# PSUM as eight single banks, a bank for fillers, an earlier identity and a new order table in a linear-attention and squared-ReLU kernel

## The chip, the cores and the metric

The kernel runs on one core of one Trainium2 chip. The metric is the device time of one execution in microseconds; the runs of the kernel before gave 358.99, 359.10 and 359.19 us, median 359.1.

## The reference

Attention with an exponential feature map and no softmax, then a feed-forward network (FFN):

```python
def phi(x):                                   # q, k: (8, 8, 576, 64), w_phi: (64, 128)
    proj = einsum('bhsd,df->bhsf', x, w_phi)
    proj = proj - max(abs(proj), axis=-1, keepdims=True)
    return concatenate([exp(proj), exp(-proj)], axis=-1)
q_p, k_p = phi(q), phi(k)
kv = einsum('bhsf,bhsd->bhfd', k_p, v)
z = sum(k_p, axis=2)
x = einsum('bhsf,bhfd->bhsd', q_p, kv) / (einsum('bhsf,bhf->bhs', q_p, z)[..., None] + 1e-06)
x = x.transpose(0, 2, 1, 3).reshape(4608, 512)
h = maximum(x @ w_in, 0.0)                    # w_in: (512, 2048)
out = (h * h @ w_out)                         # w_out: (2048, 512)
```

Inputs and output are float32; the matrix work is done in bfloat16.

## The kernel before

**Stages.** For each of the 8 batches, `k_batch` (L582) transposes k (on TensorE for batches 0 and 1, L630; by DMA transposes on the SP queue later), projects it against w_phi (L660), takes the largest magnitude per row on VectorE (L595) and both exponentials on ScalarE (L602); `em` holds the exponentials of the maxima (L704), `va` and `var` the products of v with them (L755, L738) with a column of ones beside them (L716, L720); the key-value sums go to PSUM (L776, L781) and are copied to `kvs`. `q_batch` (L811) does the same with q: transposes (L840), one projection for the maximum (L878, reduced by L925), one for the exponentials (L888, L915), the numerators and denominators (L970), their two halves added (L1009, L1013), the division (L1032, L1042), and the transpose of the result into `xT` (L1083, or by DMA).

The 36 output tiles of 128 rows are taken in chunks: four of one tile, then 16 of two. `hp_chunk` multiplies `xT` by w_in in groups of 512 PSUM columns (L1133), evicts each group with a ReLU on ScalarE (L1151) or VectorE (L1153), and squares it into `h` (L1161, L1163). `op_chunk` multiplies `h` by w_out (L1189), evicts (helper `copy`, L417 on ScalarE, L419 on VectorE) and stores each tile from the SP queue. The last tile is computed as two halves of 256 columns.

**Order.** Every operation is an `Op` with the engines that may run it. `ORDER` is a table of operation numbers, in which they are emitted; a negative number puts the operation on the second engine of its list. Each engine runs its instructions in that order. A ring (`Ring`) is a set of buffers; the table's order also decides which buffer an operation takes, and a buffer that is taken again makes the taker wait for its last reader.

**PSUM.** `r_pj` has three buffers of two banks (projections, numerators, key-value sums), `r_mo` two buffers of one bank (transposes, both FFN products, batch 0's key-value sums).

**Fillers.** `warm` (L391) issues matmuls on a constant ahead of an operation, into the buffer which that operation is about to fill; `WARM` says how many units of 128 columns, by operation number (57 in all). One operation of 40 more units stands in batch 0. 24 units on zeros open the program.

**Loads.** They are issued by GpSimd (Pool), which converts to bfloat16 on the way: first k's heads 2, 3, 6, 7 of batch 0 (`emit_heads`, L488; the others come from the SP queue as float32 and are cast), then v whole (L467), then the identity is built, the last rows of k and v (L477), and `FIRST` (q in halves L470, w_in in four parts L526), then `SECOND` (k, w_out L531, q, v). For batch 0 Pool also writes the ones of `var` (L720).

Of the kernel before, what the change touches and what calls it, by code (L numbers as in the profile page):

```python
# [17 lines left out]
ORDER = (  # L18
# [208 lines left out]
def kernel(  # L227
# [34 lines left out]


    EARLY = 2


    XB_IN, XB_X = 2, 2

# [966 lines left out]
    for o in plan.order():  # L1235
        if o.emit:
            o.emit(o)
# [30 lines left out]
```

## Time and profile before

| | |
|---|---|
| runs (median) | 359.1 us |
| span of the profiled execution | 358.4 us |
| around the span, against the median | 0.7 us |
| TensorE busy | 346.4 us, mean granted clock 0.990 |
| VectorE / ScalarE busy | 292.4 / 262.9 us |
| GpSimd busy | 58.5 us |
| first L1133 matmul, first L1189 matmul | 28.4 us, 40.1 us |
| HBM read and written | 36.77 MB, 9.44 MB |

The profiled execution's own time is given as its span. The page of the profile lists busy time by engine, slices of the span, the chain of work that ended last, and groups of instructions by source line. Line numbers in what follows are those of the kernel before, unless a changed line is meant. A row of the timeline has the start, the length, the engine, the line, the operation, output and inputs, the count of merged instructions, and in brackets the idle time ahead and what ended it.

### The profile page before, as it was taken

Reading aid. Unit: us, or ns where it says so; the run is one execution under the profiler, and the core shown is the slowest. Engines: PE = TensorE matmul, PEld = TensorE weight load, DVE = VectorE, ACT = ScalarE, POOL = GpSimd, SP = SyncE. Lnnn points to the kernel's source line nnn. Section 1 sums busy time; section 2 is a strip of 40 time slices with the busy share of each in tenths; the row PEclk is TensorE's granted clock in tenths of the full one; section 3 lists DMA queues with packets and bytes.
Section 4 is the critical chain, followed back from the end, with each engine's and each line's share of the span. In section 5 each row is a group of like instructions: output and inputs, shape, how many; then the busy total and the mean of one; then the engine's idle time right before and its main releaser. Section 6 shows DMA issues by size and latency. Waiting matters only on the chain.

```text
span 358.4 us, 9254 instructions
## 1 busy us (share of the span) xinstructions
PE 346.4 (97%) x3860; PEld 239.1 (67%) x3894; DVE 292.4 (82%) x529; ACT 262.9 (73%) x436; POOL 58.5 (16%) x88
## 2 busy tenths in 40 slices
PE   8699999999999999999999999999999999999995
PEld 4378667775776676767576757757685768576754
DVE  5979998889998998788988699979988988591310
ACT  4979997996798774698849883798879867544641
POOL 8643323442160113100220002000000000000000
PEclk9969999999999999999999999999999999999999
DMA  9999999999997499607982194435203001113011
GB/s 161 185 197 207 194 208 141 170 181 187 186 152 138 83 171 150 107 15 145 124 126 53 59 149 96 61 89 82 60 16 88 18 35 48 65 34 88 2 59 59
DMA packets 92281, 39.33 MB, mean 110 GB/s; under 512 B 59728, under 2 KB 87760, under 8 KB 92240
## 3 DMA queue, kind: packets, MB, share of 16 engines
q0 software_dynamic: 42752, 18.09, 42.7%
q1 hardware_dynamic: 49328, 20.59, 28.6%
q8 instruction: 30, 0.49, 0.6%
q10 hardware_dynamic: 160, 0.07, 0.1%
q14 instruction: 11, 0.09, 0.1%
HBM read 36.77 MB, written 9.44 MB: 129 GB/s over the span
## 4 chain that ended last, share of the span: by engine, by line
PE 82%; DVE 8%; ACT 7%; issue 1%; POOL 1%; ACTq 0%; POOLq 0%
PE mo L1133 32%; PE mo L1189 31%; PE pj L781 4%; PE pj L970 4%; ACT kph L602 4%; PE pj L878 3%; PE pj L888 2%; DVE m L595 2%; PE pj L660 2%; DVE tmp L1009 1%; ACT hr L1151 1%; PE pj L776 1%; PE mo L781 1%; DVE va L755 1%; DVE hr L1153 1%
## 5 line engine op out<-in xcount | busy, mean ns | idle before, releaser
L1133 PE MATMUL mo<-xT,win 128*128 128x256 bf16 (+1 forms) x1280 | 139.3, 262 | 0.8 <-ACT hr L1151 0.2
L1189 PE MATMUL mo<-wout,h 128*128 128x512 bf16 (+1 forms) x558 | 131.2, 373 | 1.8 <-issue 0.2
L1133 PEld LDWEIGHTS <-win 128*128 128x128 bf16 x1280 | 111.3, 98 | 19.7 <-issue 4.3
L1189 PEld LDWEIGHTS <-h 128*128 128x128 bf16 x592 | 54.5, 98 | 57.3 <-issue 2.8
L915 ACT ACTIVATE qph<-pj 128x1024 bf16<-128x1024 f32 (+1 forms) x80 | 72.8, 940 | 11.6 <-PE pj L888 11.6
L1151 ACT ACTIVATE hr<-mo 128x512 bf16<-128x512 f32 x99 | 58.7, 598 | 28.2 <-PE mo L1133 27.0
L602 ACT ACTIVATE kph<-pj 128x1024 bf16<-128x1024 f32 (+1 forms) x80 | 71.2, 949 | 6.4 <-PE pj L660 4.9
L1163 DVE TENSOR_TENSOR h<-hr 128x512 bf16<-128x512 bf16 x82 | 33.7, 419 | 22.6 <-ACT hr L1151 22.0
L925 DVE TENSOR_REDUCE mq<-pj 128x8 f32<-128x1024 f32 (+1 forms) x40 | 44.2, 1108 | 4.5 <-PE pj L878 4.4
L595 DVE TENSOR_REDUCE m<-pj 128x8 f32<-128x1024 f32 (+1 forms) x40 | 44.3, 1111 | 3.4 <-ACT kph L602 1.7
L1161 ACT ACTIVATE h<-hr 128x512 bf16<-128x512 bf16 x62 | 38.9, 631 | 8.3 <-DVE hr L1153 7.5
L755 DVE TENSOR_TENSOR va<-vin,em 128x512 bf16<-128x512 bf16 x63 | 40.2, 683 | 0.1
L1153 DVE TENSOR_SCALAR hr<-mo 128x512 bf16<-128x512 f32 x45 | 30.6, 684 | 7.9 <-PE mo L1133 7.4
L417 ACT ACTIVATE ot<-mo 128x512 f32<-128x512 f32 (+1 forms) x24 | 14.0, 585 | 25.1 <-PE mo L1189 25.1
L1009 DVE TENSOR_TENSOR tmp<-pj,e 128x520 f32<-128x520 f32 x31 | 21.1, 692 | 6.1 <-PE pj L970 6.1
L970 PEld LDWEIGHTS <-qph 128*128 128x128 bf16 x512 | 21.9, 98 | 5.4 <-issue 1.5
L1042 DVE TENSOR_TENSOR xo<-tmp,rden 128x512 bf16<-128x512 f32 (+1 forms) x39 | 24.3, 631 | 0.5
L970 PE MATMUL pj<-kvs,qph 128*128 128x65 bf16 x512 | 24.4, 194 | 0.2
L781 PEld LDWEIGHTS <-kph 128*128 128x128 bf16 x512 | 21.5, 101 | 0.3
L1013 DVE TENSOR_TENSOR tmp<-pj,tmp 128x520 f32<-128x520 f32 x31 | 21.2, 692 | 0.5 <-PE pj L970 0.4
L781 PE MATMUL pj<-va,kph 128*128 128x65 bf16 x448 | 18.4, 194 | 0.0
L467 POOL DMA_DIRECT2D vin<-in_v_dram x8 | 7.2, 895 | 68.5 <-DVE va L755 63.1
(75 smaller groups left out, 268.5 us busy)
## 6 DMA issues: line engine op xcount, KB each, us to landing
out_dram<-ot SPq DMA_DIRECT2D x31, 256.0 KB, 2.4
vin<-in_v_dram POOLq DMA_DIRECT2D x8, 512.0 KB, 9.0
kin<-in_k_dram POOLq DMA_DIRECT2D x7, 512.0 KB, 11.9
qin<-in_q_dram POOLq DMA_DIRECT2D x7, 512.0 KB, 10.3
win<-in_moe_w_in_dram POOLq DMA_DIRECT2D x4, 512.0 KB, 10.1
wout<-in_moe_w_out_dram POOLq DMA_DIRECT2D x2, 1024.0 KB, 14.8
out_dram<-ot SPq DMA_DIRECT2D x10, 128.0 KB, 2.4
xT<-xo SPq DMA_TRANSPOSE x36, 2.6
```

What stands on the lines that cost most here:

```text
L595: nc.vector.tensor_reduce(out=st["m"].rearrange("p (n c) -> p c n", c=2)[:, :, n0 : n0 + n], in_=st["pj", g][:, :, :n], axis=AX.X, op=ALU. ...
L602: nc.scalar.activation(out=st["kph"][:, s, n0 : n0 + n].rearrange("p n c f -> p c n f"), in_=st["pj", g][:, :, :n], func=ACT.Exp, scale=1. ...
L755: nc.vector.tensor_tensor(out=st["va"][:, s, gs, 0:D], in0=tiles["v", b].rearrange("p h i d -> p (h i) d")[:, gs, :], in1=st["em"][:, s, g ...
L781: nc.tensor.matmul(out=kv[:, sum_of(h) - 2 * prs[0], :], lhsT=st["kph"][:, s, 2 * h + i // 2, i % 2, :], rhs=st["va"][:, s, h * NI + i, :] ...
L915: nc.scalar.activation(out=st["qph", pt][:, s, half, n0 : n0 + n], in_=in_, func=ACT.Exp, scale=1.0 - 2.0 * s)
L925: nc.vector.tensor_reduce(out=st["mq", pt][:, half, n0 : n0 + n], in_=in_, axis=AX.X, op=ALU.max, apply_absolute_value=True)
L970: nc.tensor.matmul(out=nps[:, n + 4 * (ab or 0), :], lhsT=qph[:, s, half, sl, :], rhs=kvs[:, s, sum_of(sl), :], start=True, stop=True)
L1133: nc.tensor.matmul(out=hp[:, mi, :], lhsT=win[:, kc, mc * P : (mc + 1) * P], rhs=st_x[c][:, kc, 0:nt, :], start=kc == kcs[0] and (ab is No ...
L1151: nc.scalar.activation(out=out_, in_=in_, func=ACT.Relu)
L1153: nc.vector.tensor_scalar(out=out_, in0=in_, scalar1=0.0, scalar2=None, op0=ALU.max)
L1161: nc.scalar.activation(out=out_, in_=hr, func=ACT.Square)
L1189: nc.tensor.matmul(out=st["op"], lhsT=hst["h2"][:, mc, tt * P : (tt + 1) * P], rhs=wout[:, mc, cols], start=(mc == 0), stop=(mc == KC2 - 1))
```

## The change

PSUM becomes one ring of eight single banks, `r_ps`. A projection that took a buffer of two banks takes two banks, each with its own reductions and exponentials; the numerators are computed in groups of four heads in one bank, with sums of 260 columns; the key-value sums of every batch come in two parts. Fillers go to the first bank, which the first operation takes and which is given back by the first FFN product; they stand ahead of an operation in the order, with new counts (187 units in all), and are always matmuls of up to 512 columns.

The identity is built before any load. v of batch 0 is loaded as two halves of the heads, with k's last rows between them; the ones of `var` leave Pool for VectorE or ScalarE. w_phi comes in one transfer to both halves of the partitions, and one copy makes its bfloat16 form.

ReLU outputs of two neighbouring groups share a buffer (three of 2 x 512 instead of four of 512), and one instruction squares both; the last chunk stays as it was. The last tile is computed as 384 and then 128 columns. `load_gate` is there and not used (`GATED` is False). `ORDER` has 2078 numbers instead of 1718, all of them new; it also sets anew which engine takes the evictions, squares and copies, and the order of the loads: after batch 2's k and q, Pool issues k of batches 3 and 4 and then v of batch 2.

```diff
-    r_pj = Ring("pj", 3, [P, 2, 4, P], F32, pool=ps)
-    r_mo = Ring("mo", 2, [P, 4, P], F32, pool=ps)
+    r_ps = Ring("ps", 8, [P, 4, P], F32, pool=ps)
...
-    r_hr = Ring("hr", 4, [P, 512], BF16)
+    r_hr = Ring("hr", 3, [P, 2, 512], BF16)
...
     def c_w2(op):
-        for half in range(2):
-            rows = slice(half * Dh, (half + 1) * Dh)
-            copy(op, w2[rows, half], wst[rows])
+        copy(op, w2, wst)
...
-            nc.scalar.dma_start(out=wst[half * Dh : (half + 1) * Dh], in_=w_phi)
+        nc.scalar.dma_start(out=wst, in_=w_phi.unsqueeze(0).to_broadcast([2, Dh, Fd]))
...
     def e_first(op):
-        warm(r_pj.tile(op)[:, 0], WARM_UP, zero)
+        spare["t"] = r_ps.tile(op)
+        fill(WARM_UP, zero)
+
+    def fill(n, with_):
+        for m in [4] * (n // 4) + ([n % 4] if n % 4 else []):
+            nc.tensor.matmul(out=spare["t"][:, :m], lhsT=with_, rhs=with_.unsqueeze(1).to_broadcast([P, m, P]),
                              start=True, stop=True)
...
+            o_id.follow(after)
             o1, lb = plan.issue("sw", 2, key, {"pool": (1.7, 1.75)}, emit_heads, "kB", (), [r_in[name].slots],
-                                after=[after])
-            o3, l3 = load("v", 0, key)(o1)
-            o_id.follow(o3)
-            o2, l2 = rest(o3)
-            o2.follow(o_id)
+                                after=[o_id])
+            o_v, d_v, o = None, [], o1
+            for n in range(2):
...
+                    nc.gpsimd.dma_start(out=tiles["v", 0].rearrange("p h i d -> p h (i d)")[:, hs],
+                                        in_=v[0, hs, 0:SM, :].rearrange("h (p i) d -> p h (i d)", i=NI))
...
+                if n == 0:
+                    o2, l2 = rest(o)
...
+            for par in range(2):
+                lock = Lock()
+
+                def e_red(op, g=g, n0=n0, n=n, par=par):
+                    nc.vector.tensor_reduce(
+                        out=st["m"].rearrange("p (n c) -> p c n", c=2)[:, par, n0 : n0 + n], in_=st["pj", g, par][:, :n],
+                        axis=AX.X, op=ALU.max, apply_absolute_value=True)
...
+                        nc.scalar.activation(out=st["kph"][:, s, n0 : n0 + n, par, :], in_=st["pj", g, par][:, :n],
+                                             func=ACT.Exp, scale=1.0 - 2.0 * s)
...
+                        for hg in (0, 1) if ab is None and pt < 2 else (0,):
+                            heads = (2 * ab, 2 * ab + 1, 2 * ab + 4, 2 * ab + 5) if first_tile else range(4 * hg, 4 * hg + 4)
+                            holds = [Hold(r_ps.slots) for _ in range(1 if pt < 2 else 2)]
...
+            pair = c < len(CHUNKS) - 1
+            at, upto = (g % 2, g % 2) if pair else (0, 1)
...
+            gives += [] if chain["hp"] else [(r_ps.slots, o_first)]
...
-            wide = DM // 2 if t0 + tt == NT - 1 else DM
-            for c0 in range(0, DM, wide):
+            for c0, wide in [(0, 3 * P), (3 * P, P)] if t0 + tt == NT - 1 else [(0, DM)]:
...
     for o in plan.order():
+        if o.warm:
+            fill(o.warm, ident)
         if o.emit:
             o.emit(o)
```

More of the change, by code (lines that the diff above doesn't have):

```diff
@@ L264 @@
     EARLY = 2
-    XB_IN, XB_X = 2, 2
+    GATED = False
+    XB_IN, PE_X = 2, [(b, pt, half) for b in range(2) for pt in range(3) for half in range(2)]
     def sum_of(h):
@@ new lines, in k_batch, with e_kp @@
+        for g in groups:
+            key = kd - 6.0 - 2.2 * (4 - g)
+            holds = [Hold(r_ps.slots) for _ in range(2)]
+            def e_kp(op, g=g, holds=holds):
+                if g == 0:
+                    st["kph"], st["m"] = r_kph.tile(op), r_m.tile(op)
+                n0, n = GROUPS[g]
+                pj = [r_ps.tile(hold) for hold in holds]
+                st["pj", g, 0], st["pj", g, 1] = pj
+                for u in range(n):
+                    for par in range(2):
+                        rows = slice(par * Dh, (par + 1) * Dh)
+                        nc.tensor.matmul(out=pj[par][:, u, :], lhsT=st["kT"][rows, n0 + u, :], rhs=w2[rows, :],
+                                         start=True, stop=True)
+            o_kp = add(key - 1, {"pe": mm(P, GROUPS[g][1])}, e_kp, [cp_ops[g], o_w2],
+                       holds + ([r_kph.slots, r_m.slots] if g == 0 else []),
@@ L866, in q_batch @@
                 key = xk - 9.0 + (12 if split else 1) * pi
-                hm, hq = Hold(r_pj.slots), Hold(r_pj.slots)
-                size = 256 * w
+                hm, hq = ([Hold(r_ps.slots) for _ in range(2)] for _ in range(2))
+                banks = [(half, 4 * bank, 4) if split else (bank, n0, n) for bank in range(2)]
                 def e_qm(op, pt=pt, pi=pi, mms=mms, w=w, hm=hm):
-                    pj = st["pm", pt, pi] = r_pj.tile(hm)
+                    pj = st["pm", pt, pi] = [r_ps.tile(hold) for hold in hm]
                     if pi == 0:
                         st["mq", pt] = r_mq.tile(op)
-                    warm(pj[:, 0], op.warm)
                     for u in range(w):
@@ L877, in e_qm @@
                             rows = slice(par * Dh, (par + 1) * Dh)
[L878 to L879 removed]
+                            nc.tensor.matmul(out=pj[bank][:, u, :], lhsT=q_blocks(st, pt, blk + u, 1)[rows, 0],
+                                             rhs=w2[rows, :], start=True, stop=True)
                 def e_qp(op, pt=pt, pi=pi, mms=mms, w=w, hq=hq):
[L882 removed]
+                    pj = st["pq", pt, pi] = [r_ps.tile(hold) for hold in hq]
@@ L907, in q_batch @@
-                if split and pi:
-                    late = o_qm, o_qp
-                o_mq, o_q0 = o_mq or o_qm, o_q0 or o_qp
-                for s in range(2):
-                    def e_exp(op, pt=pt, pi=pi, half=half, n0=n0, n=n, w=w, s=s):
-                        in_ = st["pq", pt, pi][:, :, :w]
-                        if n == 8:
-                            in_ = in_.rearrange("p a b t -> p (a b) t")
-                        nc.scalar.activation(out=st["qph", pt][:, s, half, n0 : n0 + n], in_=in_, func=ACT.Exp,
-                                             scale=1.0 - 2.0 * s)
-                    exps.setdefault(pi, []).append(add(key + 2.5 + 0.2 * s, {"act": act(size)}, e_exp, [o_qp],
-                                                       give=[(r_pj.slots, hq)]))
@@ L921, in e_red @@
-                def e_red(op, pt=pt, pi=pi, half=half, n0=n0, n=n, w=w):
-                    in_ = st["pm", pt, pi][:, :, :w]
-                    if n == 8:
-                        in_ = in_.rearrange("p a b t -> p (a b) t")
-                    nc.vector.tensor_reduce(out=st["mq", pt][:, half, n0 : n0 + n], in_=in_, axis=AX.X, op=ALU.max,
-                                            apply_absolute_value=True)
-                reds.append(add(key + (3.5 if b == 0 else 0.5), {"dve": dve(size)}, e_red, [o_qm], give=[(r_pj.slots, hm)]))
+                o_qm = add(key, {"pe": mm(P, w * (1 + split))}, e_qm, need + [o_w2], hm + first[:1], give=qT_give,
+                           after=[o_mq], mode="row")
@@ new lines, in q_batch, with e_exp, e_red @@
+                o_qp = add(key + (0.1 if b else 2), {"pe": mm(128 * w, 1 + split)}, e_qp, need + [o_w2], hq + first[1:],
+                           give=qT_give, after=[o_q0], mode="row")
+                o_mq, o_q0 = o_mq or o_qm, o_q0 or o_qp
+                mine = []
+                for bank, (half_, h0, nh_) in enumerate(banks):
+                    for s in range(2):
+                        def e_exp(op, pt=pt, pi=pi, bank=bank, half_=half_, h0=h0, nh_=nh_, w=w, s=s):
+                            nc.scalar.activation(out=st["qph", pt][:, s, half_, h0 : h0 + nh_],
+                                                 in_=st["pq", pt, pi][bank][:, :w], func=ACT.Exp, scale=1.0 - 2.0 * s)
+                        exps[half_, h0, s] = add(key + 2.5 + 0.2 * s, {"act": act(128 * w)}, e_exp, [o_qp],
+                                                 give=[(r_ps.slots, hq[bank])])
+                    def e_red(op, pt=pt, pi=pi, bank=bank, half_=half_, h0=h0, nh_=nh_, w=w):
+                        nc.vector.tensor_reduce(out=st["mq", pt][:, half_, h0 : h0 + nh_], in_=st["pm", pt, pi][bank][:, :w],
+                                                axis=AX.X, op=ALU.max, apply_absolute_value=True)
+                    mine.append(add(key + (3.5 if b == 0 else 0.5), {"dve": dve(128 * w)}, e_red, [o_qm],
+                                    give=[(r_ps.slots, hm[bank])]))
@@ L1147, in e_hr, with e_hp @@
-            def e_hr(op, mcs=mcs):
-                st["hr", mcs[0]] = r_hr.tile(op, [P, gm, nt * P])
-                out_, in_ = st["hr", mcs[0]], st["hp", mcs[0]]
+            def e_hp(op, mcs=mcs):
+                hp = st["hp", mcs[0]] = r_ps.tile(op, [P, gm, nt * P], [None, None, nt * P])
+                if "h2" not in st:
+                    st["h2"] = r_h2.tile(op)
+                for mi, mc in enumerate(mcs):
+                    for kc in range(KC1):
+                        nc.tensor.matmul(out=hp[:, mi, :], lhsT=win[:, kc, mc * P : (mc + 1) * P],
+                                         rhs=st_x[c][:, kc, 0:nt, :], start=kc == 0, stop=kc == KC1 - 1)
@@ new lines, in hp_chunk @@
+            xs = [o for t in range(t0, t0 + nt) for o in x_ops[t]]
+            gives = [(r_xT.slots, xt_take[c])] if mcs[-1] == KC2 - 1 else []
+            gives += [] if chain["hp"] else [(r_ps.slots, o_first)]
+            o_hp = add(key, {"pe": mm(nt * P, 4 * gm)}, e_hp, xs + [d_win[mcs[-1] * P * WPARTS // DF]],
+                       [r_ps.slots] + ([] if o_h2 else [r_h2.slots]), give=gives, after=[chain["hp"]])
+            chain["hp"] = o_hp
+            o_h2 = o_h2 or o_hp
+            pair = c < len(CHUNKS) - 1
```

390 lines of the change are left out of this document (154 added, 236 removed), and 193 rows, old and new, of tables (ORDER, WIRE).

## The prediction

> **What bounds the kernel now.** First the page: busy shares, clock, chain.
>
> ```profile
> span 358.4 us, 9254 instructions
> PE 346.4 (97%) x3860; PEld 239.1 (67%) x3894; DVE 292.4 (82%) x529; ACT 262.9 (73%) x436; POOL 58.5 (16%) x88
> ...
> PEclk9969999999999999999999999999999999999999
> ...
> PE 82%; DVE 8%; ACT 7%; issue 1%; POOL 1%; ACTq 0%; POOLq 0%
> ```
>
> TensorE carries 82% of the chain that ended last, but its 97% includes fillers and matmuls that run slowly or wait half-filled. The clock dips in slices two and three only. So I cut the span into stretches: up to the first FFN matmul, up to where the chain becomes nearly all TensorE, and a late attention stretch.
>
> ```profile
> 0.00:28.40 28.40, 23.21 (x250) 14.72 (x250) 22.40 (x45) 20.27 (x44) 18.25 (x32) 0.88 1.29 182
> 28.40:92.00 63.60, 62.07 (x824) 43.65 (x829) 58.84 (x111) 55.11 (x94) 21.07 (x30) 1.00 1.48 182
> ...
> 172.80:246.40 73.60, 73.08 (x822) 49.92 (x829) 65.61 (x115) 55.93 (x88) 6.39 (x9) 1.00 0.56 94
> ```
>
> Columns: length, then busy time (count) of PE, PEld, DVE, ACT, POOL, clock, DMA share, GB/s. The first 28.4 us do almost no FFN work. From there to 92 us VectorE has 63.6 - 58.84 = 4.8 us free, so it paces that stretch as much as TensorE does. Later (172.8 to 246.4) VectorE has 8 us and ScalarE 17.7 us free, and TensorE sets the pace.
>
> **The start: identity first.** The timeline of all engines:
>
> ```profile
> 1.24 1.56 POOL L488 DMA_DIRECT2D kin<-in_k_dram  x2 [0.80 <-POOLq L1252]
> ...
> 3.62 0.45 DVE L419 CAST kin<-h 128x256 bf16<-128x256 f32 x1 [0.36 <-DMA h<-in_k_dram]
> 3.67 0.25 POOL masks.py:197 MEMSET ident<- 128x128 bf16 x1
> ...
> 4.00 0.29 POOL masks.py:199 TENSOR_SCALAR_AFFINE_SELECT ident<-ident 128x128 bf16<-128x128 bf16 x1
> ...
> 4.34 0.93 PE L396 MATMUL mo<-ident 128*128 128x128 bf16 x7 [0.61 <-POOL ident masks.py:199]
> ...
> 5.07 0.63 PE L630 MATMUL mo<-ident,kin 128*128 128x128 bf16 x4
> ...
> 5.49 1.24 PE L400 MATMUL pj<-ident 128*128 128x512 bf16 x3
> ...
> 6.67 0.40 PE L660 MATMUL pj<-w,kT 64*128 64x128 bf16 x8
> ...
> 7.11 1.23 DVE L595 TENSOR_REDUCE m<-pj 128x8 f32<-128x1024 f32 x1 [0.75 <-PE pj L660]
> ```
>
> k is cast by 3.62 + 0.45 = 4.07, yet its transposes start at 5.07: the identity ends at 4.29, then come seven fillers; three more (1.24 us) precede the projection. Identity first moves its 0.62 us (3.67 to 4.29) to about 1.24, and shrinks those fillers to about 0.5 us. Transposes at 4.1, copy at 4.8, projection at 5.3, reduction at 5.7: **1.4 us** earlier than 7.11. The price: k's other heads and every load queued behind them on Pool start 0.62 us later, which costs 0 to 0.62; v is now two issues around k's rows, about 0.8 us of Pool each. w_phi in one transfer and one copy is needed only by that projection, and is hidden behind the casts; uncovered it costs its one copy, at most the 0.45 of the cast.
>
> **The start: fillers in a bank of their own.** Before, each filler needed the bank of the operation that it precedes, so none could run while banks were held. Two-microsecond stretches, TensorE's timeline, then two pieces of the chain at full clock, the starts of one key-value group and the next:
>
> ```profile
> 18.00:20.00 2.00, 2.00 (x23) 1.46 (x22) 2.00 (x6) 2.00 (x9) 0.68 (x2) 0.50 1.34 202
> 20.00:22.00 2.00, 2.00 (x27) 1.80 (x27) 1.92 (x4) 1.51 (x2) 0.82 (x1) 0.50 1.24 206
> ```
>
> ```profile
> 16.66 0.93 PE L878 MATMUL pj<-w,qT 64*128 64x128 bf16 x8 [1.97 <-DVE m L595]
> ...
> 21.57 0.65 PE L781 MATMUL mo<-va,kph 128*128 128x65 bf16 x8
> ...
> 22.12 0.65 PE L781 MATMUL mo<-va,kph 128*128 128x65 bf16 x8
> ...
> 28.41 1.96 PE L1133 MATMUL mo<-xT,win 128*128 128x128 bf16 x32
> ```
>
> ```profile
> 59.09 0.06 PE pj L776
> ...
> 59.39 0.06 PE pj L776
> ```
>
> TensorE is idle for 1.97 us until a VectorE reduction frees a pair; then the granted clock is 0.50. A key-value group takes 22.12 - 21.57 = 0.55 us there, 59.39 - 59.09 = 0.30 at full clock. Six such groups lose 1.5 us, the projections and transposes between (0.93 against 0.40 for eight) about 1.5 more: 0 to 3 us. The new order has 187 units of filler (128 columns each) against 97, nearly all before the first FFN matmul, in their own bank; at 1.96 / 32 = 0.06 us a unit (L1133 above) that is 11 us, put where TensorE waits. At half clock they would be 22, and late work would queue behind them.
>
> How much of it counts is VectorE's sum. Its timeline:
>
> ```profile
> 14.03 0.68 DVE L595 TENSOR_REDUCE m<-pj 128x4 f32<-128x512 f32 x1
> 14.63 0.74 DVE L419 COPY qT<-mo 128x512 bf16<-128x512 bf16 x2
> ...
> 20.42 2.35 DVE L925 TENSOR_REDUCE mq<-pj 128x8 f32<-128x1024 f32 x2
> 23.91 0.43 DVE L419 COPY qT<-mo 128x512 bf16<-128x512 bf16 x1 [1.14 <-PE mo L840]
> 24.91 0.76 DVE L1001 TENSOR_TENSOR tmp<-pj,e 128x260 f32<-128x260 f32 x2 [0.58 <-PE pj L970]
> ...
> 27.17 0.69 DVE L1009 TENSOR_TENSOR tmp<-pj,e 128x520 f32<-128x520 f32 x1
> 27.78 0.48 DVE L419 COPY xT<-mo 128x256 bf16<-128x256 bf16 x2
> ```
>
> Before, 7.11 to 28.26 is 21.15 us, some 2.7 of them idle (1.14 and 0.58 behind slow TensorE). Steps, start to start: a 512 reduction 0.60, a 1024 one 2.35 - 1.23 = 1.12, 260 columns at most 0.38 (two in 0.76), 520 columns 0.61, a qT copy 0.74 - 0.43 = 0.31. The changed order has 12 reductions of 512 and 2 of 256, 10 products for v (0.60), 4 copies of k, 4 sums of 260, and small ones: 7.9 + 6.0 + 1.2 + 1.5 + 1.7 = 18.3 us. From 5.7 this gives 24.0 without a wait, 26.7 with the old idle time. With 1.2 us of waits and 0.5 for later loads the first FFN matmul is at 25.8: **-2.6 us**; bounds -4.4 (no waits) and -0.8.
>
> Can it be kept? The second FFN matrix decides:
>
> ```profile
> L1189 PE MATMUL mo<-wout,h x558: 272/379/391, 40.1 to 354.5; 128*128 128x512 bf16 x176, 128*128 128x256 bf16 x10
> L531 POOL DMA_DIRECT2D wout<-in_moe_w_out_dram x2: 878/885/892, 19.9 to 22.5; - x2
> ...
> DMA to landing us min/median/max: 13.4/14.8/16.1
> ```
>
> Its halves land at 33.3 to 36.0 and 35.9 to 38.6 and are first used from 40.1; 2.6 us earlier is 37.5, for the first half. It just fits.
>
> **Single banks.** Two exponentials of 1024 become four of 512, reductions and numerator sums are halved. ScalarE's prices:
>
> ```profile
> 168.07 1.02 ACT L915 ACTIVATE qph<-pj 128x1024 bf16<-128x1024 f32 x1
> ...
> 169.08 1.08 ACT L1151 ACTIVATE hr<-mo 128x512 bf16<-128x512 f32 x2
> ...
> 170.90 0.60 ACT L1151 ACTIVATE hr<-mo 128x512 bf16<-128x512 f32 x1 [0.22 <-PE mo L1133]
> ...
> 173.92 1.93 ACT L915 ACTIVATE qph<-pj 128x1024 bf16<-128x1024 f32 x2
> ```
>
> Steps: 1.08 - 0.60 = 0.48 and 1.93 - 1.02 = 0.91; a split costs 2 x 0.48 - 0.91 = 0.05 back to back, at most 0.17 by whole durations. 160 splits: 8 us (at most 27). With 26 more squares moved from VectorE (26 x 0.48) less merging, ScalarE gains about 18 us. VectorE's 80 split reductions cost 2 x 0.60 - 1.12 = 0.08 each, the 62 split sums 0.08 as well (at most 2 x 0.38 - 0.61 = 0.15): 11 us, which the moved squares (26 x 0.31, by the nearest row, the qT copies) and the merged ones give back: about 0. The table in the Trainium skill's page VectorE: DVE Perf Modes, section The TRN2 errata, charges 172 cycles at 1.2 GHz for each ScalarE read of PSUM, 0.14 us a split: 23 us by it for 8, and ScalarE would gain 33 (rival 3). The rows here show overlap back to back, so it is not taken.
>
> In exchange, FFN groups have up to eight banks, not two, and a bank is freed after one read. From 28.4 to 92 the most that can be won is VectorE's 4.8 us. From there to the last product of the fifth chunk the changed order gives VectorE 117 instructions for 95, 3.1 us more by the steps. I take **-1.0** for all up to 155 us (bounds -4.8, +3.1). Chunks 10 to 13 hold 147 ScalarE instructions against 78: 78 x 0.48 + 16 x 0.27 + 24 x 0.48 + 12 x 0.95 + 3.6 = 68 us, VectorE 70, in a stretch that takes 73.6 now. I take **+0.8** there and later (bounds -1.5, +4). The Pool order puts v of batch 2 behind k of batch 4; loads are hidden:
>
> ```profile
> L467 POOL DMA_DIRECT2D vin<-in_v_dram x8 | 7.2, 895 | 68.5 <-DVE va L755 63.1
> ```
>
> v's loads wait 63 us for buffers, so they run ahead of need. Squares over two groups come half a microsecond later, one chunk ahead of their use. The last tile ends in 128 columns, not 256: about **-0.1**.
>
> Sum: -2.6 - 1.0 + 0.8 - 0.1 = -2.9, on a span of 358.4: 355.5. The runs lie at 359.1, 0.7 above the span, so **356.2 us**.
>
> **Rivals.** (1) *Banks were the real limit*: TensorE no longer waits anywhere; -4.4 - 4.0 - 1.5 = -9.9, 349.2 us. For it: the two banks are emptied by engines that are 93 and 87% busy from 28.4 to 92. Against: those same shares leave little room, however many banks there are. Chance 0.18. (2) *The lead is lost*: the clock falls anyway, or wout lands later; only the 1.4 us of the identity less 0.6 for the loads stay, and the splits take them: 358.9 us. Chance 0.09. (3) *Slower*: ScalarE becomes a second pacer in chunks 10 to 13. It decides when instructions alternate with waits, so that whole durations count: 78 x 0.60 + 16 x 0.40 + 24 x 0.60 + 12 x 1.05 (an estimate from 0.60) + 5 = 85 us against 73.6, up to +11; half of it, less 2.6: 362 us. For it: 68 of 73.6 leaves 8% slack in a strict order; against, the steps of 0.48. Chance 0.26. (4) *Half clock in mid-kernel* from many short waits between banks: a stretch of 10 us at half clock costs 5 us, 361 us; the clock row is 9 throughout with two banks, so 0.02. That is what the Trainium skill's page TensorE: Matmul & The Clock Gate, section A second HAM failure mode: psum-queue depth-cycling, warns of for cycling banks.
>
> The forecast has 0.45. Its own range is 353 to 358.3; with the rivals the eight-in-ten range is 349 to 362.3. Faster than 359.1 by over 0.2% (about what a measurement here can tell): 0.45 + 0.18 = 0.63, and 0.01 of rival 2; same 0.08; slower 0.28.
>
> **What would show it.** First k reduction near 5.7 us; clock 1.0 from 14 to 24; first FFN matmul at 25 to 26.5, first L1159 matmul at 37 to 38.5; DVE busy near 300, ACT near 305 by whole durations; in chunks 10 to 13 no chain pieces on ScalarE longer than some 3 us. It is wrong if the clock still dips, if wout's landing ends TensorE's idle time, or if the FFN matmuls wait for ScalarE.

## The result and the profile after

The changed kernel takes 376.1 us (median of four runs, 374.4 to 378.8) where the kernel before takes 359.1: a ratio of 1.046, 95% interval 1.041 to 1.051. The forecast was 356.2. In three of the runs further down (stores_and_v2, xT_last_by_pe, half_reduce_t_late) one of the four executions was over 1.5% above the fastest; the times given leave it out, though the profile of xT_last_by_pe is of such a one. The page of the changed kernel, the lines that answer to those shown of before (span, busy time, clock by slice, shares of the chain that ended last):

```profile
span 377.0 us, 9582 instructions
...
PE 353.8 (94%) x3918; PEld 242.1 (64%) x3918; DVE 295.2 (78%) x615; ACT 278.6 (74%) x591; POOL 58.7 (16%) x87
...
PEclk9999999899999998899999999999999999999999
...
PE 56%; DVE 20%; ACT 12%; DMA 7%; issue 4%; SPq 1%; DVEq 0%; ACTq 0%
```

TensorE's busy time grew by 7 us, the span by 18.6: the rest is waiting. The chain is no longer TensorE's. VectorE and ScalarE have grown in it, and DMA, which had no share before, has 7%. The clock is whole in the start, as forecast, and dips in two new places, slices 8 and 16 to 17. By stretches, first the changed kernel, then the one of these stretches in the kernel before that tells most (length, then busy time and count of PE, PEld, DVE, ACT, POOL, then clock, DMA share, GB/s):

```profile
0.00:28.40 28.40, 25.15 (x276) 14.53 (x277) 23.36 (x51) 23.38 (x58) 18.29 (x30) 1.00 1.26 179
28.40:92.00 63.60, 59.88 (x824) 45.02 (x822) 54.78 (x119) 54.89 (x126) 18.74 (x26) 0.97 1.35 170
92.00:136.00 44.00, 42.21 (x464) 28.29 (x462) 38.33 (x76) 36.82 (x81) 7.63 (x11) 1.00 0.68 99
136.00:160.00 24.00, 16.67 (x199) 11.14 (x196) 13.71 (x33) 9.46 (x20) 4.27 (x6) 0.86 1.24 149
...
172.80:246.40 73.60, 72.47 (x828) 48.64 (x828) 67.70 (x138) 69.47 (x144) 9.77 (x14) 1.00 0.61 102
```

```profile
136.00:160.00 24.00, 23.84 (x253) 15.94 (x253) 19.25 (x33) 17.19 (x25) 2.71 (x5) 1.00 0.67 100
```

From 136 to 160 us TensorE is idle for 24 - 16.7 = 7.3 us, and VectorE, ScalarE and GpSimd are idler still; the DMA engines are busier than before (1.24 against 0.67). In the stretch that rival 3 named (172.8 to 246.4) ScalarE has 69.5 of 73.6 us, near the 68 that the forecast summed, and TensorE is idle for 1.1 us.

Equal moments are not equal work, so both traces were also lined up by work: each matmul counts with its step at full clock (0.109 us for 256 columns against win, 0.216 for 512 against wout, 0.056 for 128, 0.029 for 65, the rest in the same way; fillers and TensorE's transposes do not count), and the time at which each kernel reaches the same sum is compared. "Before" is the time in the kernel before; the other columns say how much later a kernel is there. The names are those of the runs below. Each column is one execution. With other steps for the small matmuls the rows move by 1 us or so, the first by 2; the jumps at 67 and at 136 to 144 us stay.

```
work us  before | changed  ot_four  v2_before_k4  v5_late  transposes_late  half_reduce_t_late
   10     31.1  |  -0.8      0.9       -0.9         0.8        -0.7             -0.9
   42     66.9  |  -2.0     -0.3       -2.1        -0.4        -1.9             -2.3
   50     75.9  |   2.2      0.3       -1.8        -0.1        -1.6             -2.6
   90    119.2  |   2.7      0.7       -1.4         0.5        -1.2             -3.0
  106    136.0  |   4.1      1.9        0.2         1.8         0.0             -1.5
  114    144.0  |  14.3     10.4       11.5         6.2         2.8              1.3
  202    236.9  |  16.2     15.6       13.3        11.0         5.3              3.6
  314    351.9  |  19.4     18.6       16.5        14.2         9.0              7.3
```

The changed kernel is 2.0 us ahead at 67 us. Then it loses 4.2 us at once, 1.9 up to 136, **10.2 between 136 and 144**, and 5.1 in small steps to the end (the tail gives 0.8 back). TensorE's idle time says where: after 28.4 us it is 16.8 us, in the kernel before at most 3.2. Of the 16.8, 7.6 go to copies into ot, nearly all of it behind a late store, 2.6 to the gap at 66 us, 2.4 to xT and 3.8 to results of VectorE. Two spells at half clock, 69.1 to 72.6 and 147.6 to 154.5 us, slow what runs in them.

**The 10.2 us.** Timeline of the changed kernel there:

```profile
137.67 0.90 POOL L472 DMA_DIRECT2D vin<-in_v_dram  x1 [13.77 <-DVE va L747]
137.69 3.44 SPq L584 DMA_TRANSPOSE qT<-qin  x1
141.19 2.22 SPq L1181 DMA_DIRECT2D out_dram<-ot  x2
...
150.01 0.60 ACT L423 ACTIVATE ot<-ps 128x512 f32<-128x512 f32 x1 [8.59 <-DMA out_dram<-ot]
150.66 1.87 PE L1092 MATMUL ps<-xT,win 128*128 128x256 bf16 x8 [6.70 <-ACT ot L423]
```

An output store stands on SP behind the DMA transpose of all of q of batch 4 and lands at 149.9. The copy that needs its ot buffer (one of three) waits 8.6 us, and with it the PSUM bank that TensorE's next FFN group takes. What was in flight: the DMA view of 136 to 156 us, the changed kernel, then the kernel before (issues, KB each, median us to landing):

```profile
out_dram<-ot SPq DMA_DIRECT2D x3, 256.0 KB, 6.2
...
xT<-xo SPq DMA_TRANSPOSE x5, 7.4
...
qT<-qin SPq DMA_TRANSPOSE x1, 11.0
```

```profile
out_dram<-ot SPq DMA_DIRECT2D x3, 256.0 KB, 2.9
...
xT<-xo SPq DMA_TRANSPOSE x4, 4.3
```

The new table puts the transposes of q of batch 4 (137.7) and k of batch 5 (153.8) here, beside the load of v of batch 5; the kernel before issued those two transposes at 118.6 and 124.4. TensorE first reads their results near 181 and 196 us in the changed kernel. The Trainium skill's page DMA: Bandwidth & Descriptors, section Latency and other measured facts, gives a DMA transpose an effective 261 GB/s, measured on one kernel; half a megabyte would be an estimated 2 us by it. The runs do not agree: 11.0 us in this crowd, and 4.5 for k's in the run transposes_late.

After the stall the clock falls as well:

```profile
148.00:152.00 4.00, 1.34 (x7) 0.94 (x7) 0.00 (x0) 1.99 (x5) 0.90 (x1) 0.50 1.59 176
```

The Trainium skill's page TensorE: Matmul & The Clock Gate, section HAM oscillation — how this bites in real kernels, says that a long enough wait for a DMA makes the next work start at half clock. The trace agrees: 6.7 us idle, then 0.50.

**The 4.2 us** are a gap of another kind. TensorE stops in the middle of a group of four products, with nothing to wait for; the second row is the DMA view of 66.2 to 68 us, its only packet that carries program:

```profile
68.77 0.20 PE L939 MATMUL ps<-kvs,qph 128*128 128x65 bf16 x1 [2.61 <-issue]
```

```profile
q8 instruction: 1, 0.02, 3.2%
```

In the run v2_before_k4, which has no such gap, that packet comes at 62.9 us, and TensorE reaches the same instruction near 66. Here it starts at 66.4, after TensorE had stopped at 66.2. Loads and a transpose fill the DMA engines from 58 to 68 us. The gap is 2.6 of the 4.2 us; the rest is the half clock behind it (0.50 from 70 to 72 us). That TensorE ran out of program is read from this order of events; no run isolates it. The gap is not tied to that load's place: v5_and_transposes_late, with v2_before_k4's order up to there, has one of 2.4 us, and stores_at_copy and ot_four, with the changed kernel's order, have none. So these 4.2 us need not be in every execution; the profiled one took 378.8 us, the slowest of four.

### The profile page after: what moved, and what is told of

It reads as the page before. It is cut to its first block, busy times and chain, and to the rows that moved or that the text cites. A ratio compares the mean times of both kernels' runs of the same rounds, so it can differ in the third digit from the quotient of the medians.

```text
span 377.0 us, 9582 instructions
## 1 busy us (share of the span) xinstructions
PE 353.8 (94%) x3918; PEld 242.1 (64%) x3918; DVE 295.2 (78%) x615; ACT 278.6 (74%) x591; POOL 58.7 (16%) x87
## 4 chain that ended last, share of the span: by engine, by line
PE 56%; DVE 20%; ACT 12%; DMA 7%; issue 4%; SPq 1%; DVEq 0%; ACTq 0%
PE ps L1092 25%; PE ps L1159 17%; DMA xT<-xo 3%; ACT kph L619 3%; DVE m L611 3%; DVE mq L891 3%; PE ps L769 3%; DMA out_dram<-ot 3%; ACT qph L884 3%; DVE tmp L974 2%; DVE tmp L981 2%; PE ps L408 2%; PE ps L939 2%; DVE va L747 2%; ACT h L1131 2%
## 5 line engine op out<-in xcount | busy, mean ns | idle before, releaser
L1092 PE MATMUL ps<-xT,win 128*128 128x256 bf16 (+1 forms) x1280 | 137.8, 263 | 11.2 <-ACT ot L423 7.6
L1159 PE MATMUL ps<-wout,h 128*128 128x512 bf16 (+2 forms) x592 | 138.0, 377 | 0.8 <-DVE h L1133 0.4
L1115 ACT ACTIVATE hr<-ps 128x512 bf16<-128x512 f32 x96 | 56.4, 614 | 41.6 <-PE ps L1092 35.9
L884 ACT ACTIVATE qph<-ps 128x512 bf16<-128x512 f32 (+1 forms) x160 | 78.9, 570 | 4.8 <-PE ps L870 4.7
L619 ACT ACTIVATE kph<-ps 128x512 bf16<-128x512 f32 (+1 forms) x160 | 78.4, 585 | 4.7 <-PE ps L674 3.3
L1117 DVE TENSOR_SCALAR hr<-ps 128x512 bf16<-128x512 f32 x48 | 32.6, 687 | 34.1 <-PE ps L1092 29.6
L611 DVE TENSOR_REDUCE m<-ps 128x4 f32<-128x512 f32 (+1 forms) x80 | 47.5, 628 | 4.2 <-PE ps L674 2.7
L891 DVE TENSOR_REDUCE mq<-ps 128x4 f32<-128x512 f32 (+1 forms) x80 | 47.6, 629 | 3.7 <-PE ps L861 3.4
L1131 ACT ACTIVATE h<-hr 128x1024 bf16<-128x1024 bf16 (+1 forms) x46 | 46.9, 1028 | 3.5 <-DVE hr L1117 3.0
L423 ACT ACTIVATE ot<-ps 128x512 f32<-128x512 f32 (+2 forms) x26 | 15.3, 592 | 27.4 <-PE ps L1159 17.2
L939 PE MATMUL ps<-kvs,qph 128*128 128x65 bf16 x512 | 27.0, 196 | 2.9 <-issue 2.6
```

Source lines behind the costliest of these rows:

```text
L611: nc.vector.tensor_reduce(out=st["m"].rearrange("p (n c) -> p c n", c=2)[:, par, n0 : n0 + n], in_=st["pj", g, par][:, :n], axis=AX.X, op= ...
L619: nc.scalar.activation(out=st["kph"][:, s, n0 : n0 + n, par, :], in_=st["pj", g, par][:, :n], func=ACT.Exp, scale=1.0 - 2.0 * s)
L884: nc.scalar.activation(out=st["qph", pt][:, s, half_, h0 : h0 + nh_], in_=st["pq", pt, pi][bank][:, :w], func=ACT.Exp, scale=1.0 - 2.0 * s)
L891: nc.vector.tensor_reduce(out=st["mq", pt][:, half_, h0 : h0 + nh_], in_=st["pm", pt, pi][bank][:, :w], axis=AX.X, op=ALU.max, apply_absol ...
L939: nc.tensor.matmul(out=nps[0][:, n, :], lhsT=qph[:, s, half, sl, :], rhs=kvs[:, s, sum_of(sl), :], start=True, stop=True)
L1092: nc.tensor.matmul(out=hp[:, mi, :], lhsT=win[:, kc, mc * P : (mc + 1) * P], rhs=st_x[c][:, kc, 0:nt, :], start=kc == 0, stop=kc == KC1 - 1)
```

## The experiments

Theories: (1) late stores and three ot buffers; (2) large transfers that crowd out small ones that TensorE waits for; (3) ScalarE's split exponentials, the rival on record; (4) a thin lead: too little TensorE work between the attention's last product for a chunk and the chunk's first FFN matmul; (5) VectorE's own speed. The kernel before was run again beside each group of runs, at 359.4 to 360.4 us; ratios are against those. All moves in the table go through one helper: an operation is put right behind another, the rest keeps its order, and an operation whose inputs or buffers are not there yet takes the next place where they are.

### Stores behind their copies; a fourth ot buffer

```
+                o_out, _ = plan.issue("hw", 1 + two, key, ...
+                                      give=[(r_ot.slots, o_ot)]); plan.behind.append((o_ot, o_out))
```
```
-    r_ot = Ring("ot", 3, [P, DM], F32)
+    r_ot = Ring("ot", 4, [P, DM], F32)
```

> The changed kernel with each output store put in the table right behind the copy that fills its ot buffer; nothing else moves. Theory 1 (late stores: with three ot buffers a copy waits for a store that was queued on SP far behind its own copy and then landed in a crowded moment): ScalarE's 8.6 us wait for out_dram<-ot at 141 to 150 us and TensorE's 6.7 us wait behind it disappear, the span falls from 377 by 8 to 11, so 365 to 368 us. Theory 2 (bunched loads: v of batch 2 behind k of batch 4 crowds the DMA engines, and whatever is in flight then lands late): another transfer takes the store's place, 372 to 376. Theory 3 (the halved exponentials make ScalarE the pacer): 375 to 377, no change.

> The changed kernel with four ot buffers for three; the table is as it was, so SP's queue has its order of the changed kernel. Theory 1: the copy at 141 us takes the fourth buffer and waits for nothing there; 365 to 369 us, unless a later copy meets a late store in its turn. Theory 2: the crowded moment delays transposes instead, 372 to 376. Theory 3: 375 to 377.

Measured: 381.1 us (ratio 1.059, 1.055 to 1.063) and 378.1 (1.050, 1.047 to 1.053), both above every range that was expected. The wait for the store is gone from the first and is 3.1 us in the second; another took its place. First stores_at_copy, then ot_four:

```profile
131.36 6.19 PE L1092 MATMUL ps<-xT,win 128*128 128x256 bf16 x40 [3.48 <-DMA xT<-xo]
```

```profile
153.55 0.59 PE L1092 MATMUL ps<-xT,win 128*128 128x256 bf16 x2 [6.88 <-DMA xT<-xo]
```

Theory 1 falls as the cause. The store was only the transfer that happened to be waited for: free it, and the transposed attention result (xT) is the late one. That the first run is slower because earlier stores stand ahead of the xT on SP is likely and not shown.

### v of batch 2 ahead of k of batch 4

```
+    plan.behind.append((loads["k", 3][0], loads["v", 2][0]))
```

> The changed kernel with one load moved on GpSimd: v of batch 2 ahead of k of batch 4, as in the kernel before; stores are late as in the changed kernel. Theory 2: the load leaves near 45 us and not at 58.7, the loads after 58 are less crowded, TensorE's 2.6 us gap at 66.2 goes and much of what comes later, 363 to 370 us. Theory 1: only that gap goes, if at all; the wait for the store stays, 373 to 376. Theory 3: 375 to 377.

> Both edits in one: stores behind their copies, v of batch 2 ahead of k of batch 4. Theories 1 and 2 both at work: 361 to 365 us, the gains of the two single runs added. If the time is that of one of the single runs, the other edit moves nothing of its own. Theory 3: 375 to 377.

Measured: 376.7 us (1.047, 1.043 to 1.051) and 382.4 (1.067, 1.062 to 1.073). The load order that the prediction had noticed changes nothing that can be measured. The profiled run of the first has no gap at 66 us and then the same stall of 6.8 us at 140.

### The FFN set back, or forward, in the table

```
+    place = {n: p + (40 if abs(n) in back else 0) for p, n in enumerate(seq)}
```

> The changed kernel with the FFN's operations from chunk 6 on set back by 40 places in the table (an operation takes the first later place where its inputs and buffers are there). Theory 4 (thin lead: in the changed order 4 to 9 us of TensorE work by the table's own costs lie between the last attention product that feeds a chunk and the chunk's first FFN matmul, against 9 to 14 in the order before, so that a DMA transpose of xo that lands late stops TensorE): with 40 places the distance is 6 to 21 us, the waits at 124 to 158 us go, only the 2.6 us gap at 66 and small ones stay: 360 to 367 us. Theory 2 (crowded DMA engines, whatever the lead): 372 to 377.

> v of batch 2 ahead of k of batch 4, and the FFN from chunk 6 on set back by 24 places (distance 6 to 18 us). Theory 4: between the run without a set-back (376.7) and the one with 40 places, 360 to 368. Theory 2: within 2 us of 376.7.

> v of batch 2 ahead of k of batch 4, and the FFN from chunk 6 on set back by 40 places. Theory 4: the 2 us that the start gains are kept to the end: 356 to 363 us. Theory 2: within 3 us of 376.7.

> The kernel before, nothing of the change in it, with the FFN from chunk 6 on set 32 places forward in its own table; the distance between the last attention product and the chunk's first FFN matmul falls from 9 to 14 us to 2 to 9. Theory 4: thin lead alone makes the kernel before slower, 365 to 374 us. If what costs the time is in the banks, the splits or the load order of the change, it stays at 359 to 361.

Measured: 417.9, 425.7, 418.0 and 430.7 us (ratios 1.161, 1.183, 1.161 and 1.197, each within 0.01). Every expectation missed by 38 us or more. TensorE's longest waits in before_ffn_forward32 (total, times, longest):

```profile
PE mo L1133 <- ACT hr L1151: 8.5, 12, 2.1
PE mo L1133 <- DMA xT<-xo: 7.4, 5, 5.3
PE mo L1133 <- DVE hr L1153: 6.3, 7, 1.6
```

A set-back in either direction breaks the fine interleaving: FFN groups bunch, and TensorE waits for the bank of the group just before (hr), in the kernel before too; there the clock is also at half for 31 us in mid-kernel. This says how much the planned order is worth, and leaves theory 4 undecided.

### Late loads and late transposes

```
+    plan.behind += [(loads["k", 7][1], loads["v", 5][0]), (loads["k", 7][1], loads["v", 5][1]), (loads["k", 7][1], loads["k", 6][1])]
```
```
+    plan.behind += [(plan.at[15], plan.at["k", 5]), (plan.at[15], plan.at["q", 4])]
```

> v of batch 2 ahead of k of batch 4, and three loads that leave at 137 to 141 us in the changed kernel and are first used after 195 us (v of batch 5 with its last rows, the last rows of k of batch 6) moved behind the load of k of batch 7 on GpSimd, near 177 us; every compute engine has its old order. Theory 2, now so: large transfers that nothing needs for 40 us and more run beside the small ones that TensorE waits for. This takes 0.6 MB out of 137 to 150 us: the store and xT there land in 4 us and not 7 to 8, 368 to 373 us. Theory 4 (thin lead alone: the attention results are late whatever the transfers do): 375 to 377.

> v of batch 2 ahead of k of batch 4, and the two large DMA transposes of q of batch 4 and k of batch 5 (issued at 137.7 and 153.8 us in the changed kernel, first used near 180) moved on SP's queue behind the transposes of xo for chunk 9; every compute engine has its old order. Theory 2: the stores and the xT of chunk 8 no longer stand behind or beside them, 366 to 371 us. Theory 4: 375 to 377.

> Both of these moves and v of batch 2 early. Theory 2: 137 to 158 us has stores and xT almost alone, their landings are near 2.5 us, TensorE's 10 to 11 us there go: 363 to 367 us. Theory 4: 374 to 377. If one of the two single moves gives as much, it was that transfer.

Measured: 372.0 us (1.035, 1.032 to 1.039), **369.2 (1.028, 1.025 to 1.031)** and 376.2 (1.045, 1.039 to 1.051). In transposes_late no compute engine's order differs from v2_before_k4, which took 376.7; in the two runs with v of batch 5 late, VectorE takes one reduction and one eviction ahead of its products with that v, near 210 us, and no other compute instruction moves. transposes_late, its windows and its DMA view of 136 to 156 us:

```profile
136.00:160.00 24.00, 22.01 (x199) 14.91 (x202) 17.79 (x39) 11.71 (x23) 0.86 (x2) 1.00 0.70 110
```

```profile
xT<-xo SPq DMA_TRANSPOSE x7, 5.0
...
kT<-kin SPq DMA_TRANSPOSE x1, 4.5
```

TensorE has 22.0 us of 24 where it had 16.7, the clock stays whole, and by work the kernel is 2.8 us behind at 144 instead of 11.5. The two went at 133.8 and 150.1 us in v2_before_k4 and go at 157.0 and 155.1 here. So theory 2 holds for 8.5 of the 11.3 us that v2_before_k4 loses there: two transfers of half a megabyte that nobody needs yet. v5_late alone takes more than half of it (by work 4.4 us are lost between 136 and 144 in place of 11.3); it changes nothing in SP's order of transfers, so what runs beside the small transfers counts, and not only what stands ahead of them. With both moves TensorE has 23.7 of the 24 us from 136 to 160, and yet the time, 376.2, lies in theory 4's range and not in theory 2's: the moved loads now meet chunk 10's xT, and the profiled execution has the gap of 2.4 us near 70 besides:

```profile
189.75 5.19 PE L1092 MATMUL ps<-xT,win 128*128 128x256 bf16 x24 [5.88 <-DMA xT<-xo]
```

### The same two transposes in the kernel before, and a place in between

```
+    plan.behind += [(plan.at[12], plan.at["q", 4]), (plan.at[13], plan.at["k", 5])]
```

> The kernel before, nothing of the change in it, with its DMA transposes of q of batch 4 (118.6 us) and k of batch 5 (124.4 us) moved on SP's queue to where the changed kernel has them: behind the xT of tile 12 and of tile 13, near 132 and 143 us. Compute engines keep their order. Theory 2 (the transfers suffice): 363 to 370 us. Theory 4 (they cost only where an xT is needed 3.5 us after it is issued; in the kernel before that is 5 to 9 us): 359 to 361 us.

> transposes_late with the transpose of q of batch 4 one place earlier, behind chunk 8's xT in place of chunk 9's, since in transposes_late TensorE waits 4.75 us at 161 us for the last rows of q that stand behind it. Both theories: that wait shortens by 1 to 2 us, 367 to 369; if the crowd only moves onto chunk 9's xT, 369 to 372.

Measured: 360.2 us (1.001, 0.998 to 1.003), as theory 4 had it, and 368.8 (1.024, 1.021 to 1.027). In the kernel before the two transposes went at 125 and 143 us and cost nothing, but neither did they crowd anything. Its DMA view of 132 to 156 us:

```profile
out_dram<-ot SPq DMA_DIRECT2D x3, 256.0 KB, 2.6
...
xT<-xo SPq DMA_TRANSPOSE x5, 2.5
```

The loads behind them on GpSimd moved along (q of batch 6 from 123.4 to 130.9, k of batch 6 from 134.4 to 148.3). Late transposes are not enough by themselves; that they have to meet the loads and the stores in the same few microseconds fits, and is not shown. Whether the longer lead of the kernel before would have carried it through such a crowd this run does not say. The second run's 0.4 us is within the spread of transposes_late. The 4.75 us of its expectation are a piece of the chain that VectorE waits behind: TensorE is busy for 14.9 of the 15 us from 155 to 170 in transposes_late.

### What is left: the DMA's own time, or VectorE

```
-    XB_IN, PE_X = 2, [(b, pt, half) for b in range(2) ...]
+    XB_IN, PE_X = 2, [(b, pt, half) for b in range(2) ...] + [the 15 that land last]
```
```
-  in_=st["pj", g, par][:, :n],
+  in_=st["pj", g, par][:, :n, 0:64],
-  in_=st["pm", pt, pi][bank][:, :w],
+  in_=st["pm", pt, pi][bank][:, :w, 0:64],
```

> transposes_late with the xo that lands last for each chunk from 6 on (15 of the 27 late ones and parts) transposed on TensorE and copied by VectorE, in place of the DMA transpose; 54 more transposes of 128 columns, about 3 us of TensorE. Theory 4: the waits of 1 to 2 us for xT at the starts of chunks go, more than the 3 us that it costs: 363 to 367 us for 369.2. If the attention's own chain on VectorE is late, not its transfer: 369 to 373.

> transposes_late with the reductions for m and mq taken over the first 64 of the 128 columns: 160 instructions of 0.60 us become some 0.33, about 40 us less for VectorE; the maxima are then those of half the features. Theory 5 (VectorE's late xo is what is left): 359 to 364 us for 369.2. If the DMA transposes' own time is what is left, 366 to 369.

> The changed kernel with the same halved reductions, the two transposes and v where the change puts them. Theory 5 with theory 2: VectorE's part goes, the stall at 138 to 158 us stays: 366 to 371 us for 376.1. If an earlier xo also gives the crowded transfers room enough: 359 to 365. If VectorE has no part: 373 to 377.

> The control: the kernel before with its reductions halved in the same way (80 of 1.12 us and less become some 0.6). VectorE's 4.8 free us between 28 and 92 us say that TensorE, not VectorE, sets its time: 356.5 to 359.5 us for 359.1. Under 355 would say that VectorE paces the kernel before too, and the comparison would not single out the change.

Measured: 396.1 us (1.098, 1.093 to 1.103); 370.1 (1.034, 1.030 to 1.039); 375.7 (1.045, 1.041 to 1.049); 358.1 (0.997, 0.994 to 0.999). The waits of xT_last_by_pe:

```profile
PEld L1051 <- DVE xo L1009: 14.6, 11, 2.4
PE ps L1051 <- DVE xo L1009: 10.9, 11, 2.2
PE ps L1092 <- DVE xT L425: 9.2, 8, 2.7
```

TensorE reaches the place where the transpose stood in the table 1 to 2 us before VectorE has finished xo, and an in-order engine then stands still, where the DMA queue had waited for it at no cost. The page of half_reduce_t_late (busy time, chain):

```profile
PE 348.4 (95%) x3918; PEld 239.6 (66%) x3918; DVE 260.9 (71%) x615; ACT 278.2 (76%) x591; POOL 58.7 (16%) x87
...
PE 68%; ACT 12%; DVE 9%; DMA 7%; issue 3%; SPq 0%; DVEq 0%; ACTq 0%
```

VectorE is 34 us less busy than transposes_late's 294.7, its share of the chain falls from 19% to 9%, and the median does not move (369.2 before): theory 5 falls, and with it the split reductions of the change as a cause. The profiled spans differ by 1.6 us (365.0 against 366.6), less than the 4.8 by which the runs of this kernel spread. Without theory 2's move, half_reduce_after stays at the changed kernel's time. The control gains its 1 us.

What fits a part is theory 4, on the order alone. Timelines at chunk 10, where nothing crowds: issue of its last two xT, and its first FFN matmul. First the kernel before, then the changed one:

```profile
174.42 3.93 SPq L1065 DMA_TRANSPOSE xT<-xo  x2
...
183.27 1.04 PE L1133 MATMUL mo<-xT,win 128*128 128x256 bf16 x8
```

```profile
188.70 2.50 SPq L1034 DMA_TRANSPOSE xT<-xo  x2
...
193.47 1.80 PE L1092 MATMUL ps<-xT,win 128*128 128x256 bf16 x15
```

From the second of the two issues (177.2 and 190.0 in the records) it is 6.1 us before and 3.4 after. In chunks 6 to 18 the same distance is 4.9 to 8.7 us before and 1.6 to 5.6 after (the 1.6 is chunk 13, whose first matmul starts before that last part has landed; the next is 2.7). An xT takes 2.4 us to land in the median of all 36 in the changed kernel, and up to 7.9 beside other transfers. With 3.4 us every larger disturbance is TensorE's. In the traces TensorE's work between the last attention product for a chunk and its first FFN matmul is 8 to 13 us before; after, it is 4 to 7 in ten of these 13 chunks and 9 to 14 in the others. Between them lie sums, a reciprocal, xo and the transfer, none of which a shorter reduction speeds up.

How much it is worth can be read from TensorE's own waits in transposes_late, the two longest after 28.4 us (total, times, longest):

```profile
PE ps L1092 <- DMA xT<-xo: 4.1, 4, 1.7
...
PE ps L1092 <- ACT ot L423: 1.6, 1, 1.6
```

Of 12.6 us of idle time after 28.4 us (at most 3.2 in the kernel before), 4.1 wait for xT, 1.6 for an ot buffer, 3.4 for short waits on VectorE, and 2.8 are gaps of up to 0.2 us without a visible cause. In half_reduce_t_late VectorE's part is 2.2 and that of xT 5.2. So the thin lead at xT accounts for about half of the last 8 to 9 us. That even this half is the lead's is argued, not shown: both tries to change the distance or the transfer alone broke something larger.

### Identity first, alone

```
-            o_id.follow(o3)
+            o1.follow(o_id)
+    plan.behind += [(o_go["pool"], o_id)]
```

> The kernel before with the identity made ahead of the loads on GpSimd, nothing else. By the forecast's step the first k reduction comes 1.2 to 1.4 us earlier (7.11 us in the kernel before) and the loads start 0.6 later: 358.2 to 358.9 us. If w_phi's landing, as in the changed kernel, or the loads hold the start: 359.0 to 359.8.

Measured: 359.8 us (1.000, 0.997 to 1.002), no difference. In its timeline the first reduction comes at

```profile
6.55 1.22 DVE L595 TENSOR_REDUCE m<-pj 128x8 f32<-128x1024 f32 x1 [0.99 <-PE pj L660]
```

0.56 us earlier than 7.11, not 1.2 to 1.4, and the first FFN matmul at 26.69. One profile can't tell such a step from chance: before_q4_k5_late leaves the start as it was, and its first reduction is at 6.25, its first FFN matmul at 27.18.

## Why the prediction was wrong

**The start (-2.6): at most half the size, and its gain is not shown.** In the profile shown the clock stays at 1.00, as forecast, and the first FFN matmul is at 27.15 us, 1.3 earlier than 28.41. But 13 profiles here have the changed start with its whole reductions: in eight the FFN begins at 27.1 to 27.4, in five at 28.7 to 28.9, three of these with the clock at half for 3.4 us near 7 to 11 us. The start of the kernel before, in three profiles, gives 27.2, 28.4 and 28.6, each time with the clock at half for 6.8 us between 14 and 24. So the change does end that dip, and the 1.3 us are no more than the scatter. One step that was too large is the identity's 1.4 us. The forecast's price of w_phi was "at most the 0.45 of the cast"; the timeline of the changed kernel:

```profile
5.83 0.23 DVE L425 CAST w<-wst 128x128 bf16<-128x128 f32 x1 [1.94 <-DMA wst<-in_w_phi_dram]
5.97 0.42 DVE L425 COPY kT<-ps 128x512 bf16<-128x512 bf16 x1
6.45 0.40 PE L674 MATMUL ps<-w,kT 64*128 64x128 bf16 x8 [1.67 <-DVE kT L425]
...
6.88 0.69 DVE L611 TENSOR_REDUCE m<-ps 128x4 f32<-128x512 f32 x1 [0.49 <-PE ps L674]
```

The cast waits 1.94 us for the one transfer that replaced two, and the copy of kT, ready since 4.6, stands behind it on VectorE: the reduction is 0.23 us earlier, not 1.4. The cast starts at 5.8 to 6.1 us in all 13 profiles.

**Single banks (-1.0 up to 155 us).** From the first FFN matmul to 67 us the lead grows by about 1 us, so there is no sign of harm from the bank layout itself; no run isolates it. The splits cost ScalarE (groups of the pages, the changed kernel, then the kernel before: count, busy us, mean ns):

```profile
L884 ACT ACTIVATE qph<-ps 128x512 bf16<-128x512 f32 (+1 forms) x160 | 78.9, 570 | 4.8 <-PE ps L870 4.7
L619 ACT ACTIVATE kph<-ps 128x512 bf16<-128x512 f32 (+1 forms) x160 | 78.4, 585 | 4.7 <-PE ps L674 3.3
```

```profile
L915 ACT ACTIVATE qph<-pj 128x1024 bf16<-128x1024 f32 (+1 forms) x80 | 72.8, 940 | 11.6 <-PE pj L888 11.6
L602 ACT ACTIVATE kph<-pj 128x1024 bf16<-128x1024 f32 (+1 forms) x80 | 71.2, 949 | 6.4 <-PE pj L660 4.9
```

157.3 - 144.0 = 13.3 us for 160 splits, 0.083 each by busy time; the forecast took 0.05. The Trainium skill's page VectorE: DVE Perf Modes, section The TRN2 errata, has 172 cycles at 1.2 GHz for each ScalarE read of PSUM, an estimated 0.14 us a split, which is above both. ScalarE's whole gain is 278.6 - 262.9 = 15.7 us, where the forecast had 18. Rival 3 had the right sign, but its mechanism is a small part of the loss: TensorE is idle for 1.1 of 73.6 us in the stretch from 172.8 to 246.4, and for 1.9 of 77.1 while chunks 10 to 13 run in the changed kernel (193.4 to 270.5). No ScalarE piece of the chain there is longer than 3 us; they do follow one another from 198.7 to 213.4 us, at whose end TensorE waits 0.9 us for ScalarE. No run undoes the splits.

**The step that failed is "loads are hidden".** It priced the moved transfers by the row of 63 us, and looked at GpSimd's queue only. That row is GpSimd's idle time ahead of four loads of v (7.9, 12.3, 6.6 and 36.3 us); it says when a buffer came free, not how far ahead of its use a load ran. SP's queue, whose order the new table changed as much, was not priced at all: neither where the large transposes of q and k went, nor what the small transfers behind and beside them would take. The terms "-1.0 up to 155 us" and "+0.8 there and later" therefore lacked some 10 us for the crowd at 136 to 144; 7.5 us of medians come back when two transposes are moved, with no compute engine's order changed, and this part is shown. The other 8 to 9 us by which transposes_late is still behind stay open: about half are waits for xT with a lead that the forecast did not measure. The 4 us for the program that came late are seen in the profiled execution only. The page had shown what was needed: xT's own landing time, and on the timelines how far ahead of its use each xT was issued.

**What the trace of before could not show** is how long a 256 KB store takes in such a crowd; there it was 2.4 us in the median of the whole kernel and 2.9 between 136 and 156. No rival had a transfer in mid-kernel as its mechanism.

## What to carry to other kernels

When a table of instructions is replaced, read the order of the DMA queues first: a change of buffers or banks can be neutral while large transfers that nobody needs yet land beside the small ones that the bottleneck engine waits for. Measure, for every transfer that the bottleneck waits on, the distance from its issue to its use, and hold it against its landing time in the busiest stretch, not against the median. A fix for the wait in view (another buffer, an earlier store) only shows the next late transfer; moving the large ones is what gave 7.5 us back here.

## What the runs showed of the hardware

A 256 KB store took 2.6 us to land in the median of the whole changed kernel and 6.2 between 136 and 156 us; an xT 2.4 and 7.4. In two profiles TensorE stopped for 2.4 to 2.6 us with no wait to be seen, each time with a 16 KB packet of program that started about when it stopped (66.4 against 66.2 us, 67.85 against 67.9). And a start that is the same program varies: the first FFN matmul of the kernel before came at 27.2 to 28.6 us in three profiles.
